# A linear-attention and feed-forward kernel: scores straddling two PSUM banks, copies of v as threads of their own, and a newly computed emission order

## The chip, the cores and the metric

The kernel runs on one core of one Trainium2 chip. The metric is the device time of one launch in microseconds (us). The times shown are of three runs of the kernel before; one more run was taken with the profiler on.

## The reference

Two layers, one behind the other. The first is a linear attention with a decaying state (4 batches, 8 heads, 768 tokens, head size 48); its output becomes a matrix of 3072 tokens by 384, and the second layer is a feed-forward block of 384 to 2048 to 384 with a gate:

```python
state = np.zeros((B, H, D, D))
for t in range(S):
    kt, vt, rt = k[:, :, t], v[:, :, t], r[:, :, t]
    cur = np.einsum('bhd,bhe->bhde', u[None] * kt, vt)
    y[:, :, t] = np.einsum('bhd,bhde->bhe', rt, state + cur)
    state = w[None, :, :, None] * state + np.einsum('bhd,bhe->bhde', kt, vt)
x = y.transpose(0, 2, 1, 3).reshape(B * S, H * D)
h = x @ w_in
sp = np.where(h > 20.0, h, np.log1p(np.exp(np.minimum(h, 20.0))))
out = (h * np.tanh(sp)) @ w_out
```

The two weight matrices are of 64-bit floats; the kernel gets them as pairs of 32-bit words.

## The kernel before, in words

**Tiling.** The tokens are worked on in 6 groups of 512 (128 tokens of each batch). A group takes 4 attention steps, one for each batch, 24 in all (s = 4 · group + batch), and then 16 hidden tiles of the feed-forward block (an "up" product of 128 hidden values by 512 tokens, a gate, a "down" product into three accumulators). In group 0 the first tiles are done in halves of 256 tokens, so that they can begin after two steps.

**One attention step** works on 128 tokens in chunks of 64. For the first steps, by name in the trace: `q` (L529, VectorE, called DVE) and the dots of r, u and k (L535, TensorE, called PE), copied out of PSUM as `sd` (L540, ScalarE, called ACT); the diagonal `P` built of `sd` (L564 on ACT in two halves of four instructions, or L566 on DVE); r and k scaled by powers of w (`scale`, L514, DVE); the scores of all pairs of tokens in a chunk (L586, PE) and a masked copy of them into `P` (L603, DVE); then `outputs`: P times v plus the carried state (`spread_y`, L636, in steps 0 to 3, `rows_y`, L661 and L673, from step 4 on), copied into x (L817, L821, L825). The keys are scaled by a table `TKn` (L578), which PE makes from a smaller one (`tkn`, L295; copied by ACT, L300). The first state of a batch is keys times v (`first_state`, L771 into `pa`, copied by L789); later steps update it (L754, L759). In steps 0 to 3 the fourth quarter of the head columns is laid out separately in a buffer `spread`, and that takes one copy of v a step (L720), which is named after the buffer that v lies in (`pre<-v`, `first<-v`, `pre<-vx`, `first<-vx`).

**The PSUM tile `pa`** has two banks of 512 columns. In both kernels it holds the scores, the sums of rows of `rows_y` (`straight`), the first states and the dots. Four PE passes of different steps thus write to the same two banks.

**The weights** arrive as 16 pieces of raw words (`wraw`), 8 of each matrix. Each piece is converted by one ACT instruction (L402) and three of DVE (L406, L408, L410), and later split into a high and a low part (L426 on ACT, L428 on DVE) for products in three passes (L892). Tiles ahead of the split use the whole value (L1014 up, L1028 down).

**What sets the order.** All engines run what the program hands them in the order in which it was emitted. A planner, the class `Flow`, computes this order when the kernel is built: each piece of work is a thread, a generator that yields names of events to wait for and costs on an engine. The planner keeps a time for each engine and takes what is ready first; among what gets ready within a margin (`PATIENCE`), a thread of a lower rank goes first if its rank is below `URGENT`. Ranks of attention steps come from `rank(s)`, those of weights from the tile that first needs them, less a lead (`L_IN`, `L_OUT`, `LAG`). `CONVERT` gives the ranks of the first conversions, `X_SPLIT` that of splitting x, `W_SHIFT` shifts the ring of weight buffers, `LO0` and `HI0` set where steps are placed among the tiles of group 0, `FETCH` the planner's price of an instruction fetch on PE. Where the planner sees PE without work, it emits filler matmuls (`keep_warm`, L310, the name `idle` in the trace), and 23 more stand at the start.

The line numbers in this section and in the prediction's quoted rows are those of the kernel before; in the kernel after, lines from 318 on stand 1 lower, those of `outputs` and what follows 7 (L586 is L587 there, L771 is L778, L1014 is L1021).

Of the kernel before, what the change touches and what calls it, by code (L numbers as in the profile page):

```python
# [21 lines left out]
B, H, S, D = 4, 8, 768, 48  # L22
NP = H // 2
C = 128
CK = C // 2
# [3 lines left out]
KT = DM // 128  # L29
# [23 lines left out]
FB = 2  # L53
COLS = FB * T
W_SLOTS = 17
W_SHIFT = 6
N_CST = CK + CK // 2


# [12 lines left out]
def split_early(w):  # L72
    return not w[0] and WG * w[1] >= FROM


def first_use(c):
    return UNITS.index((0, c) if c < AHEAD else (None, WG * c))
# [12 lines left out]
LAND0, LAND = 3.8, dict(rk=1.32, v=0.66, raw=1.96, rkn=0.5)  # L90
HT = 2 * C
FROM = 10
X_SPLIT = 0
CONVERT = (-999.5, -998.5)
LAG = 6
LO0, HI0, LO1, HI1 = 0.0, 0.85, 0.05, 0.85
LAT, LAT0 = 0.15, 0.13
WARM0, WARM_MIN, FILL = 23, 0.25, 3.25
DMA_LAT = 2.0
BLOCK0, BLOCK, FETCH, LOADING = 449, 256, 6.0, 18.0  # L100
PATIENCE = dict(dve=0.1, act=0.1, pe=0.1)
URGENT = -900
RANK = dict(token_table=-998.6, keys=-998.9, first_state=-899.5)

COST = dict(dve=1.5)
FREE = dict(pe=8.0, act=4.5, dve=2.0, pool=1.7, sp=1.0)

L_ATT, L_V, L_IN, L_OUT, L_GATE, L_EVAC, L_PUT, L_FIN = 2, -2, 7, 5, 2, 4, 9, 4


class Flow:
# [56 lines left out]
    def run(self):  # L168
        while self.live:
# [5 lines left out]
            t, th, d = min(todo[e], key=lambda t: (t[0], t[1][0]))  # L175
            soon = [o for o in todo[e] if o[0] <= t + PATIENCE.get(e, 0.0) and o[1][0] < min(th[0], URGENT)]
            if soon:
# [15 lines left out]
def act(cols):  # L193
    return {"act": 0.1 + cols / 1060}
# [6 lines left out]
def pe(us, n):  # L201
    us = Us(us)
    us.n = n
    return {"pe": us}
# [3 lines left out]
def rwkv_mish_kernel(ctx, tc, rkT, rkN, vN, wT, w_in, w_out, consts, rkF, vF, wF, uF, outT):  # L208
    nc = tc.nc
# [38 lines left out]
    loaded, marks = {}, {}  # L248
# [31 lines left out]
    spread = (pre[:, 1], pre2)  # L280
# [22 lines left out]
    flow = None  # L303

    def keep_warm(n, out=None):

        if flow:
            flow.begun += 2 * n
        for _ in range(n):
            nc.tensor.matmul(  # L310
                idle if out is None else out, lhsT=zeros.broadcast_to([128, 128]),
                rhs=zeros.broadcast_to([128, 512]), start=True, stop=True,
            )

    pa = ps.tile([128, 2, 512], F32, name="pa", tag="pa")
    for i in range(2):
        keep_warm(1, pa[:, i])
    scored = pa[:, :, : NP * CK].rearrange("j i (p t) -> j i p t", p=NP)
    straight = pa[:, :, NP * CK : (NP + 2) * CK].rearrange("m i (q t) -> m i q t", q=2)
    first_states = [pa[:, b, NP * CK : NP * (CK + D)].rearrange("d (p e) -> d p e", p=NP) for b in range(2)]  # L320
    dotted = pa[:, 0, NP * (CK + D) : NP * (CK + D) + H]
    idle = ps.tile([128, 512], F32, name="idle", tag="acc0")
    keep_warm(WARM0 - 2)

    flow = Flow(FREE, 2 * WARM0)
# [48 lines left out]

    W_ORDER = sorted(((i, f) for i in range(2) for f in range(NW)), key=lambda w: first_use(w[1]) + w[0] * W_SHIFT)
    S_ORDER = sorted(W_ORDER, key=lambda w: not split_early(w))
# [232 lines left out]
    def spread_y(s):  # L609
        rk, _, v = loaded[s][:3]  # L610
        P = Ps.pop(s)
        ys = ps.tile([128, 512], F32, name="y", tag="yt"), hp_tile("yh", f"half{s}")
        todo = [[], []]

        def add(row, j, b, k, lhsT, rhs):
            todo[row].append((j, (2 * k + b) * CK, lhsT, rhs))

        for q in range(NP) if s >= 2 else ():
            for b in range(2):
                for k in (q,) if q < KT else range(KT):  # L620
                    for j in range(2):
                        i, p = head(q, j)
                        at = 2 * (s % 2) + b
                        S = states[ROWS[i], at, p] if q < KT else spread_S[ROWS[i], at, j, k]
                        add(i, j, b, k, S, rk[ROWS[i], 0, p, HALVES[b]])
        for n in range(2 * KT):
            for j in range(2):
                for b in range(2):
                    i, p = head(min(n, KT), j)
                    lhsT = v[HALVES[b], j, n] if n < KT else spread[s % 2][HALVES[b], j, n - KT]  # L630
                    add(b, j, b, n % KT, lhsT, P[HALVES[b], 2 * p + i])
        for n in range(max(map(len, todo))):
            for row in range(2):
                if n < len(todo[row]):
                    j, at, lhsT, rhs = todo[row][n]
                    nc.tensor.matmul(  # L636
                        ys[row][HALVES[j], at : at + CK], lhsT=lhsT, rhs=rhs, start=n < 2, stop=n >= len(todo[row]) - 2
                    )
        return ys
# [55 lines left out]
    reads = [0] * NS  # L695
    stamp = const.tile([1, 1], F32, name="stamp")

    def outputs(s):
        rows, last = s >= B, s >= NS - 2
        yield f"masked{s}"  # L700
        yield f"v{s}"
        if s:
            yield f"y{s - 1}"
        if s >= 2:
            yield f"state{s - 2}"
        if rows:
            if not last:
                yield f"keys{s}"
                yield f"state{s - 1}"
            if s + 1 < NS:  # L710
                yield f"scaled{s + 1}"
            yield from hp_free()
        else:
            if s >= 2:
                yield f"out{s - 2}"
                yield f"spread{s - 2}"
            yield from hp_free()
            engine = yield {**act(96), "dve": 0.25}
            v = loaded[s][2]
            (nc.scalar.copy if engine == "act" else nc.vector.tensor_copy)(  # L720
                out=spread[s % 2][:, :, :, D:], in_=v[:, :, KT, :D].rearrange("t q (k e) -> t q k e", k=KT)
            )
        yield from paced(s, 1)
        if not rows:
            yield pe(*((0.95, 96) if s < 2 else (1.8, 192)))
            yield from hp_free(0.0)
            ys = spread_y(s)
        else:
            yield pe(2.1 - 0.4 * last, 256 - 64 * last)
            yield from hp_free(0.0)  # L730
            ys = rows_y(s, last)
        flow.set(f"out{s}")
        flow.start(finish(s, ys), rank(s) - L_FIN)
        if not rows:
            flow.start(first_state(s), s + (RANK["first_state"] if s < 2 else -899.5))
        elif not last:
            yield from update_state(s, new_states(ys))
        else:
            flow.set(f"state{s}")
# [3 lines left out]
    def new_states(ys):  # L743
        return [y[:, 2 * CK : 2 * CK + NP * D].rearrange("d (p e) -> d p e", p=NP) for y in ys[::-1]]
# [121 lines left out]
    def paced(s, piece):  # L866
        if s >= B:
            yield f"u{place(s, piece)}"

    def rank(s):  # L870
        return (place(s, 0) if s == B else place(s - 1, 1)) - L_ATT if s >= B else s - 1000
# [7 lines left out]
    def hp_free(cost=None):  # L879

        if cost is None:
            if len(hp_log) >= 2:
                yield hp_log[-2]
            return
        while len(hp_log) >= 2 and hp_log[-2] not in flow.events:
            yield hp_log[-2]
            yield pe(cost, 0)
# [299 lines left out]

    load_early()
    for s in range(NS):
        for k, thread in enumerate((load_step, load_v, scale, dots, diag, keys, attend, outputs)):  # L1190
            if thread is keys and s >= NS - 2 or s <= B and thread in (load_step, load_v):
                continue
            if thread is keys and s < B:
                flow.start(keys(s), s + (RANK["keys"] if s < 2 else -899.8), 0.0)
                continue
            flow.start(thread(s), rank(s) + k / 1000 - (L_V if s >= B and thread is load_v else 0), 0.0)
    flow.start(check_range(), 999, 0.0)
    flow.start(split_x(), X_SPLIT, 0.0)
    flow.start(load_rest(), -1200, 0.0)
    flow.start(prologue(), -1100, 0.0)  # L1200
    flow.start(token_table(), RANK["token_table"], 0.0)
    for c in range(len(W_ORDER)):
        i, f = W_ORDER[c]
        at = first_use(f) + (LAG - L_OUT if i else -L_IN) + c / 1000
        flow.start(convert(c), CONVERT[c] if c < len(CONVERT) else at, 0.0)
    for n, (i, f) in enumerate(S_ORDER):
# [12 lines left out]
    with tc.If(in_range < 128 * N_FLAGS):  # L1219
# [48 lines left out]
        with tc.tile_pool(name="any2", bufs=1) as work:  # L1268
            raw = work.tile([128, WE, 2], U32, name="raw")
            top, bottom = raw[:, :, 1], raw[:, :, 0]  # L1270
            e = work.tile([128, WE], F32, name="e")
            eu = e.bitcast(U32)
            for c, key in enumerate(W_ORDER):
# [7 lines left out]
                    out=eu, in0=top, scalar=0x80000000, in1=eu, op0=ALU.bitwise_and, op1=ALU.bitwise_xor  # L1281
# [10 lines left out]
            for b in range(B):  # L1292
                with tc.For_i(0, S, 128) as t0:
# [4 lines left out]
                    t = ps.tile([128, 512], F32, name="t", tag="yt")  # L1298
                    for k in range(KT):
                        nc.tensor.transpose(  # L1300
                            out=t[:, k * 128 : (k + 1) * 128], in_=xt[:, k].rearrange("t q e -> t (q e)"), identity=unit32
                        )
                    t = t[:, : KT * 128].rearrange("m (k t) -> m k t", k=KT)
# [81 lines left out]
```

## Time and profile before

| | us |
|---|---|
| median of 3 runs | 495.22 (495.0 to 495.71) |
| the profiled run | 494.16 |
| span in its profile, first to last instruction | 492.1 |
| PE busy | 480.5 (98% of the span) |
| ACT busy | 399.0 (81%) |
| DVE busy | 364.9 (74%) |
| first large up tile on PE starts at | 25.77 |
| first three-pass tile | 74.04 |
| first up tile of group 1 | 106.78 |

Times within a profile count from the start of the span. PE is busy nearly throughout; a lower clock of PE counts as busy too, and so does a filler matmul. "Granted clock" is the share of full speed that the chip's throttle gave PE in a stretch.

### The profile page before, as it was taken

How to read it: one execution, taken by the hardware profiler on the slowest of the kernel's cores; microseconds unless marked ns; L12 is line 12 of the kernel's file. 1: busy time of each engine (PE TensorE's matmuls, PEld its weight loads, DVE VectorE, ACT ScalarE, POOL GpSimd, SP SyncE). 2: the span in 40 equal slices, each digit the busy share in tenths (PEclk: the TensorE clock that was granted, in tenths of full speed). 3: DMA queues.
4: the chain of work that ended last, by engine and by line, in shares of the span. 5: the costliest groups of instructions: out<-in, count | busy, mean ns of one | idle time of the engine just before them, and what ended most of it. 6: DMA issues, size and time to landing. Idle time of an engine off the chain costs nothing.

```text
span 492.1 us, 11411 instructions
## 1 busy us (share of the span) xinstructions
PE 480.5 (98%) x4869; PEld 385.9 (78%) x4870; DVE 364.9 (74%) x584; ACT 399.0 (81%) x506; POOL 5.3 (1%) x28
## 2 busy tenths in 40 slices
PE   8899999999999999999999999999999999999993
PEld 4688878866678888888888888888888888888872
DVE  7899999996998665779787788875878546554531
ACT  3668999899898888886869596989787888989881
POOL 2000000000000000000000000000000000000000
PEclk9789999999999999999999999999999999999998
DMA  8792694510244030236042446142435112120002
GB/s 328 278 334 91 239 311 162 207 38 5 95 148 128 3 111 1 98 117 214 10 148 93 162 143 215 46 143 99 163 111 195 66 37 108 65 104 24 3 0 71
DMA packets 19979, 60.45 MB, mean 123 GB/s; under 512 B 3088, under 2 KB 3984, under 8 KB 19920
## 3 DMA queue, kind: packets, MB, share of 16 engines
q1 hardware_dynamic: 17184, 54.80, 32.8%
q10 hardware_dynamic: 2736, 4.84, 2.7%
q8 instruction: 40, 0.66, 0.5%
q14 instruction: 19, 0.16, 0.1%
HBM read 52.94 MB, written 4.72 MB: 117 GB/s over the span
## 4 chain that ended last, share of the span: by engine, by line
PE 93%; ACT 3%; DVE 2%; issue 1%; DMA 0%; ACTq 0%; DVEq 0%
PE hp L892 36%; PE acc L892 30%; PE acc L1028 9%; PE hp L1014 6%; PE pa L586 3%; PE yt L661 1%; PE yh L771 1%; PE pa L673 1%; PE pa L661 1%; PE pa L535 1%; PE idle L310 1%; PE yh L673 1%; PE y L636 1%; PE acc L1148 1%; ACT L919 1%
## 5 line engine op out<-in xcount | busy, mean ns | idle before, releaser
L892 PE MATMUL hp<-x,w 128*128 128x512 f32 x720 | 180.7, 395 | 0.0
L892 PEld LDWEIGHTS hp<-x,w 128*128 128x128 f32 x720 | 133.8, 188 | 30.3 <-issue 2.4
L892 PE MATMUL acc<-gh,w 128*128 128x512 f32 x468 | 156.1, 389 | 0.0
L892 PEld LDWEIGHTS acc<-gh,w 128*128 128x128 f32 x468 | 87.8, 188 | 18.3
L892 PE MATMUL acc<-gl,w 128*128 128x512 f32 x234 | 91.1, 390 | 0.0
L932 DVE TENSOR_TENSOR hb<-hb,fa 128x1024 f32<-128x1024 f32 x40 | 48.9, 1222 | 54.9 <-ACT fa L925 54.8
L919 ACT ACT_TABLE_LOAD x48 | 61.6, 1283 | 6.5 <-DVE hb L932 5.1
L925 ACT ACT_TABLE_LOAD x48 | 61.6, 1283 | 0.8
L919 ACT ACTIVATE fa<-hb,small 128x1024 f32<-128x1024 f32 x48 | 55.3, 1153 | 1.5 <-DVE hb L932 0.8
L922 ACT ACTIVATE fa<-fa 128x1024 f32<-128x1024 f32 x48 | 50.9, 1061 | 0.9
L892 PEld LDWEIGHTS acc<-gl,w 128*128 128x128 f32 x234 | 43.9, 188 | 9.5 <-DVE gl L940 0.4
L925 ACT ACTIVATE fa<-fa 128x1024 f32<-128x1024 f32 x48 | 50.9, 1060 | 0.5
L940 DVE TENSOR_TENSOR gl<-hb,gh 128x1024 fp32r<-128x1024 f32 x40 | 48.9, 1221 | 1.7 <-ACT gh L936 1.1
L1080 ACT COPY hb<-hp 128x512 f32<-128x512 f32 x55 | 32.2, 585 | 20.9 <-PE hp L892 15.2
L1080 DVE COPY hb<-hp 128x512 f32<-128x512 f32 x41 | 28.3, 690 | 25.2 <-PE hp L892 23.7
L1028 PE MATMUL acc<-gf,wraw 128*128 128x256 f32 (+1 forms) x144 | 44.4, 453 | 0.0
L1028 PEld LDWEIGHTS acc<-gf,wraw 128*128 128x128 f32 x144 | 27.9, 196 | 10.5 <-issue 7.7
L936 ACT CAST gh<-hb 128x1024 fp32r<-128x1024 f32 x14 | 14.7, 1053 | 20.0 <-DVE hb L932 19.9
L1014 PE MATMUL hp<-x,wraw 128*128 128x256 f32 (+1 forms) x108 | 28.9, 420 | 0.0
L514 DVE TENSOR_TENSOR rk<-rk,TRK 112x1024 f32<-112x1024 f32 x22 | 26.8, 1220 | 0.6 <-DMA rk<-in_rkT_dram 0.6
L1014 PEld LDWEIGHTS hp<-x,wraw 128*128 128x128 f32 x108 | 21.5, 204 | 4.3 <-issue 1.9
L936 DVE CAST gh<-hb 128x1024 fp32r<-128x1024 f32 x26 | 18.0, 694 | 2.3 <-PE acc L892 0.2
(140 smaller groups left out, 569.5 us busy)
## 6 DMA issues: line engine op xcount, KB each, us to landing
wraw<-in_w_in_dram SPq DMA_DIRECT2D x16, 768.0 KB, 4.5
wraw<-in_w_out_dram SPq DMA_DIRECT2D x16, 768.0 KB, 4.7
rk<-in_rkT_dram SPq DMA_DIRECT2D x22, 512.0 KB, 4.5
rkn<-in_rkN_dram SPq DMA_DIRECT2D x20, 384.0 KB, 4.8
v<-in_vN_dram SPq DMA_DIRECT2D x22, 256.0 KB, 4.9
out_dram<-ob ACTq DMA_DIRECT2D x12, 256.0 KB, 2.2
x<-x SPq DMA_DIRECT2D x60, 32.0 KB, 1.9
out_dram<-we ACTq DMA_DIRECT2D x5, 256.0 KB, 4.8
```

The costliest lines, as they stand in the source:

```text
L514: marks[f"scaled{s}"] = nc.vector.tensor_tensor(out=rk[:112].rearrange("d a p (b t) -> d (a p) b t", b=2), in0=rk[:112].rearrange("d a p ( ...
L586: nc.tensor.matmul(scored[h, i, p], lhsT=rk[ROWS[i], 1, p, h], rhs=rk[ROWS[i], 0, p, h], start=True, stop=True)
L892: nc.tensor.matmul(out, lhsT=a, rhs=m, start=first and n == 0, stop=last and n == 2)
L919: nc.scalar.activation(o.g, o.hb, AF.Sigmoid, bias=bias_ln2, scale=1.0)
L922: nc.scalar.activation(o.g, o.g, AF.Arctan)
L925: nc.scalar.activation(o.g, o.g, AF.Sin, scale=2.0)
L932: nc.vector.tensor_tensor(out=o.hb, in0=o.hb, in1=o.g, op=ALU.mult)
L936: (nc.scalar.copy if engine == "act" else nc.vector.tensor_copy)(out=o.gh, in_=o.hb)
L940: nc.vector.tensor_tensor(out=o.gl, in0=o.hb, in1=o.gh.bitcast(F32), op=ALU.subtract)
L1014: nc.tensor.matmul(hp[:, at], lhsT=whole[0, f // WG][:, fs], rhs=xs[0][:, k, steps, 0], start=k == 0, stop=k == KT - 1)
L1028: nc.tensor.matmul(accs[mt][:, at], lhsT=whole[1, f // WG][:, ws], rhs=g[:, of], start=not n and not i, stop=n == NF - 1, skip_group_check ...
L1080: (nc.scalar.copy if engine == "act" else nc.vector.tensor_copy)(out=o.hb[:, j], in_=h)
```

## The change

Four edits. First, the columns of `pa`: each bank is seen as two quarters of 256 columns. The scores go to the second quarter of bank 0 and the first of bank 1, which lie next to each other, 512 columns in one piece; row sums and first states go to the outer quarters, the dots from bank 0 to the end of bank 1. Second, the copy of v into `spread` in steps 0 to 3 is taken out of `outputs` and made a thread, which can go as soon as v is there and the buffer is free. Third, constants of the planner. Fourth, with these the order of emission comes out anew.

```diff
-W_SHIFT = 6
+W_SHIFT = 4
...
-X_SPLIT = 0
-CONVERT = (-999.5, -998.5)
+X_SPLIT = 4
+CONVERT = (-998.4, -997.4, -996.4, -995.4)
...
-LO0, HI0, LO1, HI1 = 0.0, 0.85, 0.05, 0.85
+LO0, HI0, LO1, HI1 = 0.05, 0.80, 0.05, 0.85
...
-BLOCK0, BLOCK, FETCH, LOADING = 449, 256, 6.0, 18.0
+BLOCK0, BLOCK, FETCH, LOADING = 449, 256, 4.5, 18.0
...
-URGENT = -900
+URGENT = 1000
...
-L_ATT, L_V, L_IN, L_OUT, L_GATE, L_EVAC, L_PUT, L_FIN = 2, -2, 7, 5, 2, 4, 9, 4
+L_ATT, L_V, L_IN, L_OUT, L_GATE, L_EVAC, L_PUT, L_FIN = 3, -2, 8, 6, 2, 4, 9, 4
...
-    scored = pa[:, :, : NP * CK].rearrange("j i (p t) -> j i p t", p=NP)
-    straight = pa[:, :, NP * CK : (NP + 2) * CK].rearrange("m i (q t) -> m i q t", q=2)
-    first_states = [pa[:, b, NP * CK : NP * (CK + D)].rearrange("d (p e) -> d p e", p=NP) for b in range(2)]
-    dotted = pa[:, 0, NP * (CK + D) : NP * (CK + D) + H]
+    quarters = pa.rearrange("j i (h c) -> j (i h) c", h=2)
+    scored = quarters[:, 1:3].rearrange("j i (p t) -> j i p t", p=NP)
+    straight = quarters[:, ::3, : 2 * CK].rearrange("m i (q t) -> m i q t", q=2)
+    first_states = [quarters[:, 3 * b, : NP * D].rearrange("d (p e) -> d p e", p=NP) for b in range(2)]
+    dotted = quarters[:, 3, NP * D : NP * D + H]
...
+    def spread_v(s):
+        if s >= 2:
+            yield f"out{s - 2}"
+        yield f"v{s}"
+        engine = yield {**act(96), "dve": 0.25}
+        v = loaded[s][2]
+        (nc.scalar.copy if engine == "act" else nc.vector.tensor_copy)(
+            out=spread[s % 2][:, :, :, D:], in_=v[:, :, KT, :D].rearrange("t q (k e) -> t q k e", k=KT)
+        )
+        flow.set(f"spread_v{s}")
+
     def outputs(s):
...
+            yield f"spread_v{s}"
             if s >= 2:
-                yield f"out{s - 2}"
                 yield f"spread{s - 2}"
             yield from hp_free()
-            engine = yield {**act(96), "dve": 0.25}
-            v = loaded[s][2]
-            (nc.scalar.copy if engine == "act" else nc.vector.tensor_copy)(
-                out=spread[s % 2][:, :, :, D:], in_=v[:, :, KT, :D].rearrange("t q (k e) -> t q k e", k=KT)
-            )
...
     for s in range(NS):
+        if s < B:
+            flow.start(spread_v(s), rank(s) + 0.0045, 0.0)
```

Where the order changes, three places count. The first is PE just behind the outputs of step 0, before (the last matmul of those outputs, `P` times `pre`; the table `tkn`; dots and scores of step 2; the outputs of step 1):

```order
L636 MATMUL yh<-P,pre 64x64
L295 MATMUL tkn<-pre,TRK 64x96 x8
L535 MATMUL pa<-cst,q 128x2 x4
L586 MATMUL pa<-first 64x64 x16
L636 MATMUL y<-P,v 64x64
L636 MATMUL yh<-P,v 64x64
```

In the new order the table stands ahead of step 0's outputs, and behind them come scores 1, dots 2 and the first state of step 0 (`pa<-v,kn`), then fillers:

```order
L637 MATMUL yh<-P,pre 64x64
L587 MATMUL pa<-rk 64x64 x16
L536 MATMUL pa<-cst,q 128x2 x4
L778 MATMUL pa<-v,kn 48x48 x16
L310 LDWEIGHTS zeros
L310 MATMUL idle<-zeros 128x512
```

First state 0 has moved from behind the dots of step 3 to here, and the scores of step 2 have gone from here to behind step 1's outputs. The number of fillers between step 0's scores and the first up tile falls from 11 to 7.

The second place is PE around the first up tile (`hp<-x,wraw`), before. Here stand the dots of step 3, first state 0 and the scores of step 3, and the tile behind them:

```order
L636 MATMUL yh<-P,first 64x64
L535 MATMUL pa<-cst,q 128x2 x4
L771 MATMUL pa<-v,kn 48x48 x16
L586 MATMUL pa<-first 64x64 x16
L1014 MATMUL hp<-x_285,wraw 128x256 x6
L636 MATMUL y<-first,S 64x64
```

In the new order scores 2 and dots 3 come first, and the scores of step 3 stand behind the tile:

```order
L637 MATMUL yh<-P,first 64x64
L587 MATMUL pa<-first 64x64 x16
L536 MATMUL pa<-cst,q 128x2 x4
L1021 MATMUL hp<-x_267,wraw 128x256 x6
L587 MATMUL pa<-first 64x64 x16
L637 MATMUL y<-first,S 64x64
```

So the tile no longer stands behind the scores of step 3, nor directly behind the first state.

The third place is ACT from the copy of the table `TKn` on, before (dots copy `sd` and diagonal `P` of step 2, a weight conversion, the outputs of step 1 into x, the dots copy of step 3, the first state):

```order
L300 COPY TKn<-tkn 128x384
L720 COPY first<-v 128x6x16
L540 COPY sd<-pa 128x8
L564 ACTIVATE P<-cst,sd 128x64 x8
L402 ACTIVATE wraw<-wraw 128x768
L817 COPY x_285<-y 128x3x64
L817 COPY x_285<-yh 128x3x64
L540 COPY sd<-pa 128x8
L789 COPY S<-pa 112x4x48
L402 ACTIVATE wraw<-wraw 128x768
```

In the new order the table's copy stands between the halves of step 1's diagonal, and the conversion and the state copy between the halves of step 2's:

```order
L565 ACTIVATE P<-cst,sd 128x64 x4
L300 COPY TKn<-tkn 128x384
L565 ACTIVATE P<-cst,sd 128x64 x4
L824 COPY x_267<-y 128x3x64
L705 COPY pre<-vx 128x6x16
L824 COPY x_267<-yh 128x3x64
L541 COPY sd<-pa 128x8
L403 ACTIVATE wraw<-wraw 128x768
L565 ACTIVATE P<-cst,sd 128x64 x4
L796 COPY S<-pa 112x4x48
L565 ACTIVATE P<-cst,sd 128x64 x4
```

The copies of v that stood behind the table's copy have moved ahead; the state copy `S<-pa` now stands ahead of step 1's copies into x, in the middle of step 2's diagonal.

The first group's later part has two more moves on PE: hidden tile 8 and one set of down products stand ahead of step 4 instead of behind it, and the first tile in three passes (`hp<-xp,w`) ahead of step 5 instead of behind it. On DVE the split of that tile's weights (L428) stands directly behind step 4's state update. From the second group on PE's order is the same, but for a small matmul of the check on the weights' range, which moves by one tile; the last part of the order is the same on PE, ACT and DVE.

## The prediction

> **What bounds the kernel now.** I read the page first, then the busy time in stretches, then the rows of the first 40 us engine by engine. The page of the kernel before gives the span, the share of TensorE (PE), its slices, the granted clock, and the chain that ended last:
>
> ```profile
> span 492.1 us, 11411 instructions
> PE 480.5 (98%) x4869; PEld 385.9 (78%) x4870; DVE 364.9 (74%) x584; ACT 399.0 (81%) x506; POOL 5.3 (1%) x28
> ...
> PE   8899999999999999999999999999999999999993
> ...
> PEclk9789999999999999999999999999999999999998
> ...
> PE 93%; ACT 3%; DVE 2%; issue 1%; DMA 0%; ACTq 0%; DVEq 0%
> ```
>
> PE is busy for 480.5 of 492.1 us, and the chain is PE for 93%. So time can only be won where PE stands idle, does filler work, or runs at a lower clock. The first three slices and the last show all of that there is. The order of the tail is unchanged by the edit, so the start decides. In stretches of 3.4 us the start reads as follows (columns: stretch and its length, then busy time and count of PE, weight loads, DVE, ACT, POOL, then the granted clock, DMA share, GB/s); the last row is the rest of the first token group:
>
> ```profile
> core 0: us, PE busy (x) PEld busy (x) DVE busy (x) ACT busy (x) POOL busy (x), PEclk, DMA share, GB/s
> 0.70:4.10 3.40, 3.15 (x8) 1.19 (x9) 0.93 (x4) 1.49 (x2) 3.27 (x3) 1.00 0.61 198
> ...
> 7.50:10.90 3.40, 2.83 (x49) 2.35 (x49) 3.37 (x7) 1.27 (x6) 0.00 (x0) 1.00 1.05 402
> 10.90:14.30 3.40, 3.40 (x12) 1.47 (x12) 3.40 (x6) 3.37 (x15) 0.00 (x0) 0.50 1.02 408
> 14.30:17.70 3.40, 3.40 (x106) 2.78 (x104) 3.34 (x7) 2.11 (x6) 0.00 (x0) 0.99 0.74 274
> 17.70:21.15 3.45, 1.94 (x83) 1.64 (x82) 2.94 (x6) 2.44 (x11) 0.00 (x0) 1.00 0.66 233
> 21.15:24.55 3.40, 2.69 (x40) 2.52 (x40) 2.09 (x3) 1.01 (x4) 0.00 (x0) 0.50 0.85 257
> 24.55:27.95 3.40, 3.24 (x37) 2.77 (x38) 2.38 (x5) 1.94 (x6) 0.00 (x0) 0.50 0.94 374
> ...
> 26.00:123.00 97.00, 97.00 (x1276) 76.24 (x1277) 90.62 (x148) 85.68 (x120) 0.44 (x5) 0.99 0.49 171
> ```
>
> Two things stand here. First, from 26 us on PE is never idle (97.00 of 97.00). Second, the clock is whole or half in steps of 3.4 us, and it follows the busy share of the stretch before: after 3.15 and 3.40 busy it is whole; after 2.83, 1.94 and 2.69 it is half; after 3.24 it is whole from 27.95 on. I use that as this trace's rule: over about 3.1 of 3.4 us busy, the next stretch is whole.
>
> The PE rows between step 1 and the first big tiles (start, length, then the instructions, then idle time ahead of them and its cause):
>
> ```profile
> 10.22 1.20 PE L535 MATMUL pa<-cst,q 112*128 112x2 f32 x8
> 11.28 3.60 PE L310 MATMUL idle<-zeros 128*128 128x512 bf16 x9
> 14.81 0.69 PE L586 MATMUL pa<-rk 48*64 48x64 f32 x32
> 15.32 0.22 PE L636 MATMUL y<-P,v 64*64 64x64 f32 x1
> ...
> 16.13 0.88 PE L295 MATMUL tkn<-pre,TRK 112*64 112x96 f32 x16
> 16.94 1.05 PE L535 MATMUL pa<-cst,q 112*128 112x2 f32 x8
> 17.93 0.69 PE L586 MATMUL pa<-first 48*64 48x64 f32 x32
> ...
> 19.20 0.27 PE L636 MATMUL yh<-P,v 64*64 64x64 f32 x1 [0.49 <-issue]
> ...
> 21.73 1.87 PE L535 MATMUL pa<-cst,q 112*128 112x2 f32 x8 [1.61 <-DVE P L603]
> 23.53 0.90 PE L771 MATMUL pa<-v,kn 64*48 64x48 f32 x32
> 24.71 1.14 PE L586 MATMUL pa<-first 48*64 48x64 f32 x32 [0.28 <-ACT sd L540]
> 25.77 3.93 PE L1014 MATMUL hp<-x,wraw 128*128 128x256 f32 x12
> ...
> 31.79 5.46 PE L1014 MATMUL hp<-x,wraw 128*128 128x256 f32 x24
> ...
> 38.96 2.87 PE L1014 MATMUL hp<-x,wraw 128*128 128x256 f32 x12
> ```
>
> From 11.28 to 14.81 PE does nine filler matmuls, .39 us each at half clock. At 21.73 the dots of step 3 have waited 1.61 us for step 2's masked copy. Dots, first state, scores and part of the first up tile then run at half clock (dots 1.87 against 1.05 at 16.94; the tile 3.93 against 2.87). Tiles 1 and 2 start at 31.79; from there PE runs through in both kernels, so I measure the change at that point.
>
> ACT and DVE around it:
>
> ```profile
> 13.24 1.06 ACT L564 ACTIVATE P<-cst,sd 128x64 f32<-128x64 bf16 x4
> ...
> 17.06 0.48 ACT L300 COPY TKn<-tkn 128x384 f32<-128x384 f32 x1 [0.27 <-PE tkn L295]
> ...
> 18.69 0.17 ACT L540 COPY sd<-pa 128x8 f32<-128x8 f32 x1 [0.98 <-PE pa L586]
> ...
> 20.81 0.89 ACT L402 ACTIVATE wraw<-wraw 128x768 f32<-128x768 uint32 x1
> ```
>
> ```profile
> 17.07 0.68 DVE L529 TENSOR_TENSOR q<-first 112x512 f32<-112x512 f32 x1
> 17.67 0.55 DVE L578 TENSOR_TENSOR kn<-kn,TKn 128x384 f32<-128x384 f32 x1
> 18.14 0.95 DVE L408 SCALAR_TENSOR_TENSOR we<-wraw,we 128x768 uint32<-128x768 uint32 x1
> ...
> 20.94 0.73 DVE L603 COPY_PREDICATED P<-cst,pa 128x512 f32<-128x512 uint32 x1 [0.51 <-ACT P L564]
> 21.57 1.21 DVE L514 TENSOR_TENSOR first<-first,TRK 112x1024 f32<-112x1024 f32 x1
> ```
>
> **The change part by part.** *New columns.* The scores, the state products and the dots still lie in the two banks of one tile, and they stay ordered by bank: after the change the copy of the dots still waits for the scores, as at 18.69 (0.98, released by the scores, which write other columns than it reads). Worth 0; at most the 0.28 of 24.71, at least 0, since no pass is added.
>
> *Copies of v as threads.* Four copies of 96 columns either way; three on ACT and one on DVE before and after. They come earlier, where ACT waits for its first dots. Worth 0.
>
> *Constants.* They matter through the order. From the second group on PE's order is the same but for the one small matmul of the range check. In the first group tile 8 and the first three-pass tile come earlier against steps 4 and 5; PE is busy there throughout and its matmuls are the same, so 0, while ACT and DVE keep up (the rival below prices it).
>
> *The start.* Four fillers fewer (11 become 7 after step 0's scores), the token table ahead of step 0's outputs, first state 0 and the dots of step 3 earlier, scores 3 behind the first up tile. I walk the new order with the rows above, start to start:
> - PE: dots 1 as before to 11.3; 3 fillers at half clock 1.2 (12.5); table, half clock, some 1.3 (13.8); 2 fillers .6 (14.4); outputs 0 .81 (15.2); scores 1 .51 (15.7); dots 2 .99 (16.7); first state 0, .6 (17.3), since 0.90 was at half clock. Its keys need the table's copy, 13.8 + .48, then .47 on DVE: 14.8, in time.
> - DVE's masked copy 1 now waits for that first state: 17.35 + .63 = 18.0. ACT: dots copy 18.2, weight conversion .83 (19.05), half of the diagonal .96 (20.0), state copy .3 (20.3). PE's scores 2 wait for that state copy, in the same banks: 20.35 to 20.9. Queued on DVE behind the masked copy: scale 2 1.15, keys .47, a shift .46, q 3 .60, to 20.7. Dots 3 start at 20.9; from 21.15 at half clock, since the stretch 17.70 to 21.15 holds about 1.9 us of PE work (outputs 1, with its .49 stall, then a gap of 1 us): 1.75, to 22.65.
> - Up tile 0 starts at 22.65 against 25.77. The stretch 21.15 to 24.55 is now full of PE work (dots 3, then the tile), 3.3 to 3.4 us instead of 2.69, so by the rule the clock is whole from 24.55, not 27.95. The tile is 2.84 us of whole-clock work (2.18 us at half clock and 1.75 whole before): 1.90 us at half speed do .95, the other 1.89 end at 26.45.
> - Scores 3 .5 (26.95); their scaled keys are due at 22.7 + .63 + .95 + 1.15 = 25.4, in time. Outputs 2 and first state 1 took 31.79 − 29.70 = 2.09: tiles 1 and 2 start at 29.05.
>
> The gain is 31.79 − 29.05 = 2.7 us. It splits into 1.9 from an earlier first tile with scores 3 behind it, and .85 from the earlier whole clock. Before's profiled run took 494.16 us (2.06 around its span), 1.06 under the median of the three runs shown. The sum, 494.16 − 2.7 = 491.4 against that run, is 492.5 against the median 495.22.
>
> **A rule of the skill against the trace.** Half clock here follows stretches with gaps of at most 1.61 us. The Trainium skill, "TensorE: Matmul & The Clock Gate", section "Why this matters for your kernels", says that drops are avoided when no idle gap of PE exceeds about 3 us; by it the new start would never fall to half clock. The same page of the Trainium skill, Part 1, tells of a free-running window of about 3.4 us, and with that the trace agrees (steps of 3.4 us); on the gap it doesn't, since 2.83 busy of 3.40, with no gap over half a microsecond, was already followed by half clock.
>
> **The rivals.**
> 1. *The clock stays whole throughout.* Speaks for it: the fillers and the earlier work could lift the stretch before 21.15 over the mark. Against: my walk has 1.9 us busy there. Then dots 3 end at 21.9, the tile at 24.8, and masked copy 3 on DVE (27.05) holds first state 1: tiles 1 and 2 at 27.7, gain 4.1, time 491.1. By the Trainium skill's gap rule just named this would be the case.
> 2. *Half clock until 27.95 as before*, because eight dots of two columns don't count as busy, or the steps lie elsewhere against the program. For: 2.69 busy, mostly dots and first state, was not enough. Against: 3.24 was, and the new stretch has more. Then the tile ends at 28.15, tiles 1 and 2 start at 30.75: gain 1.0, time 494.2.
> 3. *Half clock in 14.30 to 17.70 too*, since five fillers and the table replace nine fillers. PE's 3.1 us of work from 14.3 then end 1.7 later, at 19.0, and all behind it shifts: dots 3 end near 24.8, the tile at 29.3, tiles 1 and 2 at 31.8: gain 0, time 495.2. Against: 10.90 to 14.30 has no gap in my walk.
> 4. *It doesn't do what it says.* The columns free no wait (as at 18.69), and the reordered waits on the banks (masked copy 1 for first state 0, scores 2 for the state copy) cost what they save: 495.2.
> 5. *Slower: the first three-pass tile waits.* It now stands ahead of step 5 on PE, about 2.0 us of PE work earlier, besides the 2.7. These rows show its weights made on DVE and its use:
>
> ```profile
> 69.65 0.95 DVE L428 TENSOR_TENSOR w<-wraw,w 128x768 fp32r<-128x768 f32 x1
> ...
> 74.04 2.20 PE L892 MATMUL hp<-xp,w 128*128 128x512 f32 x8
> ```
>
> The tile would be due at 74.04 − 4.7 = 69.3. Were the weights made as late as now (70.6), PE would wait 1.3 of the 2.7 gained. It decides from weights at 72.0; at 73.0 the kernel is .2% slower, 496.2. For it: DVE idles only 6.4 of 97 us, and must also do more of the conversions. Against: DVE's new order puts that split right behind step 4's state update, near 66.
>
> **How the numbers follow.** A change of .2%, 1.0 us, is about what can be told from none. Chances: forecast .50 (492.5), rival 1 .07 (491.1), rival 2 .15 (494.2, on the line between faster and same), rival 3 .11, rival 4 .08 (both 495.2), rival 5 .09 (496.2 or more). Faster: .50 + .07 + half of .15 = .65. Same: the other half + .11 + .08 = .26. Slower: .09. The range leaves out rival 5 and half of rivals 3 and 4 above (.19) and little below: 491.1 to 495.2. The forecast's own range is 491.9 to 493.2 (.6 either way for the handoffs that I read at under .1 us each).
>
> **What would show it.** Right: the first up tile starts near 22.7 and tiles 1 and 2 near 29; the clock is half only in 10.9 to 14.3 and 21.2 to 24.6; 7 fillers after step 0's scores; no wait of PE before the dots of step 3 on a masked copy, but one of about 1 us before scores 2, released by ACT's state copy; PE without idle time in the rest of the first group; same tail. Wrong: half clock at 25 to 28 (rival 2) or 15 to 17 (rival 3), PE waits before the first three-pass tile (rival 5), or a start as late as before.

## The result, and the profile after

The change made the kernel slower: 499.66 us (median of 20 runs, 494.2 to 501.88) against 496.05 us before (20 runs, 494.38 to 497.52), a ratio of 1.0061 with a 95% interval of 1.0043 to 1.008. I had forecast 492.5 us, faster. The profiled run of the changed kernel took 495.84 us, one of its quicker ones, so its trace holds the causes but less than their usual cost. Ratios and their intervals, here and below, are as recorded and not the quotients of the medians; they leave out slow runs, those over 1.5% above the fastest of their kernel (501.88 here, 544.76 us with 40 instructions more, 806.15 us with one load earlier).

The waits of PE in the changed kernel (what waited and for what: us in total, times, longest):

```profile
PE hp L1021 <- issue: 3.3, 1, 3.3
PE pa L310 <- DVE small L233: 0.9, 1, 0.9
PE pa L536 <- DVE q L530: 0.7, 1, 0.7
PE yh L637 <- issue: 0.6, 1, 0.6
...
PE pa L587 <- ACT S L796: 0.2, 1, 0.2
```

The wait for step 2's masked copy (1.61 us before) is gone, and one of 3.3 us has taken its place, ahead of an up tile, released by nothing that the trace shows ("issue"). The PE rows of the start show where it lies:

```profile
14.50 0.65 PE L587 MATMUL pa<-rk 48*64 48x64 f32 x32
15.08 1.05 PE L536 MATMUL pa<-cst,q 112*128 112x2 f32 x8
16.06 0.58 PE L778 MATMUL pa<-v,kn 64*48 64x48 f32 x32
...
20.33 1.05 PE L536 MATMUL pa<-cst,q 112*128 112x2 f32 x8
21.26 2.87 PE L1021 MATMUL hp<-x,wraw 128*128 128x256 f32 x12
24.29 0.70 PE L587 MATMUL pa<-first 48*64 48x64 f32 x32 [0.17 <-issue]
27.04 0.58 PE L778 MATMUL pa<-v,kn 64*48 64x48 f32 x32 [0.42 <-DVE P L604]
30.90 8.34 PE L1021 MATMUL hp<-x,wraw 128*128 128x256 f32 x24 [3.29 <-issue]
40.97 2.87 PE L1021 MATMUL hp<-x,wraw 128*128 128x256 f32 x12
```

The new start is fast: the first up tile begins at 21.26 (25.77 before), first state 1 ends at 27.6. Tiles 1 and 2 could follow 4 us earlier than before's 31.79. PE stands until 30.90 instead, and then the two tiles take 8.34 us (5.46 before). The stretches of this run, cut where its clock steps, show why (columns as before):

```profile
9.49:12.90 3.41, 2.67 (x54) 2.06 (x55) 2.99 (x6) 2.72 (x12) 0.00 (x0) 1.00 1.06 417
12.90:16.32 3.42, 3.42 (x120) 2.79 (x119) 3.37 (x5) 2.54 (x11) 0.00 (x0) 1.00 1.03 404
16.32:19.73 3.41, 1.97 (x82) 1.33 (x72) 2.96 (x5) 2.20 (x8) 0.00 (x0) 1.00 0.54 149
19.73:23.14 3.41, 3.41 (x49) 3.19 (x50) 2.93 (x5) 2.36 (x10) 0.00 (x0) 1.00 0.40 164
...
26.56:29.97 3.41, 0.64 (x35) 0.45 (x32) 3.38 (x7) 1.91 (x5) 0.00 (x0) 1.00 0.88 300
29.97:33.38 3.41, 2.48 (x6) 2.03 (x7) 3.10 (x5) 1.38 (x3) 0.00 (x0) 0.50 1.00 416
33.38:36.80 3.42, 3.42 (x10) 2.71 (x9) 1.38 (x2) 0.37 (x1) 0.00 (x0) 0.50 1.02 416
```

After the stretch with .64 us of PE work the clock is half for two stretches. A gap of 3.3 us and some 3 us of slower tiles outweigh the 4 us won.

All runs list their span and mean granted clock, and that separates the two causes. Span times clock is the span as if the half-clock time had run at full speed; it varies little, while the rest of the spread is half-clock time, 2 · (1 − clock) · span. The split is rough, since a clock that is half while PE stands counts too:

| kernel | span x clock, mean us | time at half clock, median us |
|---|---|---|
| before (runs beside the experiments) | 486.5 to 486.9 | about 14 |
| changed (20 runs; 12 more) | 488.6; 488.9 | 17.9; 16.9 |

So about 2 us of the loss (1.7 to 2.4) are idle time or work, and about 2 us (half of some 4 us) are clock. For example a run of 494.2 us had a clock of .991 (8.9 us at half), one of 501.55 us one of .979 (21 us).

### The profile page after: what moved, and what is told of

Its sections match the earlier page's. It is cut to its first block, busy times and chain, and to the rows that moved or that the text cites. A ratio compares the mean times of both kernels' runs of the same rounds, so it can differ in the third digit from the quotient of the medians.

```text
span 493.9 us, 11405 instructions
## 1 busy us (share of the span) xinstructions
PE 479.3 (97%) x4864; PEld 385.3 (78%) x4866; DVE 363.7 (74%) x580; ACT 399.3 (81%) x510; POOL 5.3 (1%) x28
## 4 chain that ended last, share of the span: by engine, by line
PE 90%; ACT 3%; DMA 2%; DVE 1%; issue 1%; SPq 0%; ACTq 0%; DVEq 0%
PE hp L899 36%; PE acc L899 30%; PE acc L1035 8%; PE hp L1021 6%; PE pa L587 2%; DMA rk<-in_rkT_dram 1%; PE yt L662 1%; PE yh L778 1%; PE pa L674 1%; PE pa L662 1%; DMA wraw<-in_w_in_dram 1%; PE yh L674 1%; PE pa L536 1%; PE acc L1155 1%; ACT L926 1%
## 5 line engine op out<-in xcount | busy, mean ns | idle before, releaser
L899 PE MATMUL hp<-x,w 128*128 128x512 f32 x720 | 180.8, 396 | 0.0
L899 PEld LDWEIGHTS hp<-x,w 128*128 128x128 f32 x720 | 133.9, 188 | 30.2 <-issue 2.1
L899 PE MATMUL acc<-gh,w 128*128 128x512 f32 x468 | 156.2, 389 | 0.0
L899 PEld LDWEIGHTS acc<-gh,w 128*128 128x128 f32 x468 | 87.9, 188 | 18.2
L899 PE MATMUL acc<-gl,w 128*128 128x512 f32 x234 | 91.2, 390 | 0.0
L899 PEld LDWEIGHTS acc<-gl,w 128*128 128x128 f32 x234 | 43.9, 188 | 9.5 <-DVE gl L947 0.4
L1087 DVE COPY hb<-hp 128x512 f32<-128x512 f32 x40 | 27.6, 690 | 23.0 <-PE hp L899 21.4
L1021 PE MATMUL hp<-x,wraw 128*128 128x256 f32 (+1 forms) x108 | 30.9, 442 | 3.3 <-issue 3.3
L1021 PEld LDWEIGHTS hp<-x,wraw 128*128 128x128 f32 x108 | 22.6, 215 | 8.1 <-issue 5.3
L352 DVE TENSOR_REDUCE small<-we 128x1 f32<-128x768 f32 x16 | 15.2, 949 | 10.9 <-ACT we L350 10.9
```

The source lines that it names most:

```text
L352: v.tensor_reduce(out=to[:, 0:1], in_=e, axis=AX.X, op=ALU.min)
L899: nc.tensor.matmul(out, lhsT=a, rhs=m, start=first and n == 0, stop=last and n == 2)
L1021: nc.tensor.matmul(hp[:, at], lhsT=whole[0, f // WG][:, fs], rhs=xs[0][:, k, steps, 0], start=k == 0, stop=k == KT - 1)
```

## The experiments

Three explanations stood against each other: F, the gap is the fetch of PE's instructions; W, it is a wait of the program that the profile misnames; B, the new columns cost time in every step. For F speaks a row of the DMA records: in a window of 1.1 us in the gap there is one packet of 16 KB on the instruction queue, and none in the 6 us ahead of it (queue and kind: packets, MB, share):

```profile
q8 instruction: 1, 0.02, 5.6%
```

If an instruction takes 64 bytes, 16 KB are 256 of them, the planner's own `BLOCK`; the runs below test that. The 40 packets of this queue in the whole run would make 10240 instructions, about as many as the profile counts of PE (9730).

**The changed kernel once more.**

> The changed kernel once more, for a second profile. Theory F (instruction fetch): the start of the new order is as fast as walked, but PE then stands for 2 to 5 us ahead of up tiles 1 and 2 with no releaser in the trace, until a 16 KB packet of the instruction queue has landed about 1.3 us before; the gap lets the clock fall, and the spread of the runs is time at half clock (about 10 us of it in a run of 496, about 18 to 21 us in a run of 499 to 501). Rival W: the gap is a wait of the program that the profile fails to name (a weight's conversion, a copy into x). Rival B: the two-bank columns cost time in every step.

Measured: 499.06 us (12 runs), ratio 1.0062 (1.0034 to 1.0089). In its profile the gap is there, 2.32 us, after a start that was 1.7 us later. As F has it.

**The columns alone.** The diff of the columns, as shown, on the kernel before.

> The kernel before with the new columns of the PSUM tile alone; its order of emission is the same, instruction for instruction. Theory F: no difference, ratio 1.000 within 0.002. Rival B: slower by the 3.6 us that the whole change lost, or a good part of them.

Measured: 496.38 against 495.83, ratio 1.0016 (1.0005 to 1.0027). Not the 3.6 us that were lost, so B falls as the main cause; but not quite nothing either.

**84 more instructions ahead of everything.**

```diff
-    keep_warm(WARM0 - 2)
+    keep_warm(WARM0 - 8)
+    for _ in range(48):
+        nc.tensor.matmul(idle[:, :32], lhsT=zeros.broadcast_to([128, 128]),
+                         rhs=zeros.broadcast_to([128, 32]), start=True, stop=True)
```

> The changed kernel, with 6 of the 21 wide filler matmuls at the very start replaced by 48 narrow ones (32 columns) of about the same time together: 42 matmuls and their weight loads, 84 PE instructions, more ahead of everything, and nothing else moved. Theory F: the borders of the instruction blocks (256 instructions of 64 bytes) come 84 instructions earlier in the program, the block with up tile 1 is asked for 2 to 3 us earlier (during the first up tile instead of behind it), and the gap ahead of tiles 1 and 2 shrinks from 3.3 to under 1.5 us or vanishes; time 3 to 6 us less than the changed kernel's 499.7. Rival W: the gap stays at 3 us where it is, time 499 to 500.

Measured: 494.02 us, ratio .9958 (.9941 to .9975): 5 us less than the changed kernel, with more filler instructions in about the same time. Span times clock falls from 488.9 to 485.4. Its PE rows show no gap ahead of the tiles:

```profile
32.72 0.56 PE L782 MATMUL pa<-v,kn 64*48 64x48 f32 x28
33.20 5.46 PE L1025 MATMUL hp<-x,wraw 128*128 128x256 f32 x24
```

**A whole block more.** The same with 15 wide fillers out and 143 narrow ones in, 256 instructions.

> The changed kernel with 15 of the wide fillers at the very start replaced by 143 narrow ones (32 columns): 128 matmuls with their weight loads, 256 PE instructions, more, one whole block of instructions, so that the borders of the blocks stand where they stand without any shift. Theory F (borders of blocks of 256): the gap ahead of tiles 1 and 2 is back, 2 to 3.5 us; span times clock back at 488 to 489; time 497 to 501. Rival N (not the borders but something else about the narrow fillers, such as an earlier first matmul or a warmer clock, made shift84 5 us faster): no gap, 493 to 495.

Measured: 500.33 us, ratio 1.0068 (1.0038 to 1.0098). The gap is back in its place, and with it span times clock (488.4):

```profile
32.52 0.56 PE L782 MATMUL pa<-v,kn 64*48 64x48 f32 x28
36.81 7.14 PE L1025 MATMUL hp<-x,wraw 128*128 128x256 f32 x24 [3.73 <-issue]
```

That the effect has a period of 256 instructions, and that the narrow fillers by themselves help nothing, is the clearest evidence for F. A count of PE's instructions in the traces (matmuls, weight loads and those of its sequencer, in order of their start) says the same. Each gap that F claims, in this run and the others, stands ahead of an instruction within two of the 449th or the 961st, which are two blocks apart. At the 449th are .49 us in the kernel before, .62 in the changed one and .66 with 40 more; at the 961st 3.29 in the changed one, 2.32 in its second profile and 1.71 with 40 more. With 256 more the latter gap stands at the 1219th, a block further on. The planner's constants `BLOCK0, BLOCK = 449, 256` put the borders there too.

**Forty instructions more** (3 wide out, 23 narrow in), to see whether the gap moves with the border.

> The changed kernel with 3 wide fillers replaced by 23 narrow ones: 20 matmuls with their weight loads, 40 PE instructions, more. Theory F: the border that lay right ahead of tiles 1 and 2 now lies 40 instructions earlier, which is inside first state 1 (64 instructions, which end there): the gap starts after about 12 of its 32 matmuls and no longer behind them; it is asked for at nearly the same time (scores 3 lie there, dense), so its length stays 2 to 3.5 us, time 497 to 501. Rival W (a wait of tiles 1 and 2): the gap stays directly ahead of the tiles.

Measured: the gap is inside first state 1, after 4 + 8 = 12 of its 32 matmuls, as forecast:

```profile
32.55 0.24 PE L782 MATMUL pa<-v,kn 64*48 64x48 f32 x1
...
32.73 0.37 PE L782 MATMUL pa<-v,kn 64*48 64x48 f32 x8
34.81 0.47 PE L782 MATMUL pa<-v,kn 64*48 64x48 f32 x20 [1.71 <-issue]
35.21 5.46 PE L1025 MATMUL hp<-x,wraw 128*128 128x256 f32 x24
```

Nothing in the profile ties the thirteenth of these matmuls to anything, so W falls. Its length, 1.71, is under the 2 to 3.5 that I gave, and so is the time, 496.63 us, ratio 1.0004 (.9985 to 1.0022).

**The shift on the kernel before.**

> The kernel before with the 84 additional PE instructions of shift84. Theory F: there the block came just in time (its packet had landed at 30.1, tiles 1 and 2 began at 31.8), and PE was held by other waits, so that little is to be won: 495 to 496, ratio 0.998 to 1.001. Rival N: the shift alone gives what shift84 gained over the kernel before, 493.5 to 494.3. Possible loss under F: a border falls in another dense stretch, up to 3 us.

Measured: 496.57 against 496.1, ratio .9998 (.9982 to 1.0014). The shift is worth nothing there; what it frees in the changed kernel is the changed order's own gain.

**The shift with old columns,** and **128 instructions with old columns** (8 wide out, 72 narrow in), and **the changed kernel with old columns.**

> shift84 with the old columns of the two-bank tile; the order of emission is the same. Where the columns do nothing: 494.0, the same as shift84. Where they cost what the comparison with the columns alone suggests (ratio 1.0016): 493.2.

> The changed kernel with old columns and 128 more PE instructions (8 wide fillers become 72 narrow). Theory F: the border lies inside the outputs of step 2, asked for before the first up tile; the gap is under 1 us, and time is 492 to 494, as with 84. If the earlier border now meets another dense stretch: a gap of 1 to 2 us there, 494 to 496.

> The changed kernel with the old columns; order of emission the same. Columns inert: 499.5 +- 0.7. Columns costing 0.8 us as between shift84 and its twin: 498.5. The gap ahead of tiles 1 and 2 stays.

Measured: 493.02 us, ratio .9937 (.9914 to .996), the best of all; 494.05, ratio .9959 (.9944 to .9974), no gap, the time just above the 492 to 494 given; 498.73, ratio 1.004 (1.0009 to 1.0071), gap 4.19 us. In the last one the profile names a releaser for the gap:

```profile
PE hp L1020 <- ACT first L801: 4.2, 1, 4.2
```

The tile doesn't read what that copy writes, and in the changed kernel the same copy ran at 31.79, after the tile had begun: a coincidence of time. The gap stands ahead of the 961st instruction here too.

**The planner's price of a fetch.** `FETCH` back from 4.5 to 6.0 in the changed kernel.

> The changed kernel with one constant undone: the planner's price of an instruction fetch back at 6.0 from 4.5; the order is computed anew, and in it the first up tile stands behind the outputs of step 2 instead of ahead of them. Theory F: the planner then counts with the gap that the trace shows (fetch to resumption some 5 to 6 us) and puts other work in it; PE's gap is smaller, 494 to 497, faster than the changed kernel. Rival: the gap stays ahead of the next tiles and costs the same, 499 to 500.

Measured: 497.96 us, ratio 1.0035 (1.0017 to 1.0054), just outside the range given, and 1.7 us under the changed kernel. The fetch gap is gone, but PE waits in other places:

```profile
PE hp L1021 <- ACT hb L1087: 2.4, 1, 2.4
PE pa L587 <- ACT S L796: 2.1, 1, 2.1
```

**The copies of v alone.** `spread_v` and its start, as in the diff, on the kernel before.

> The kernel before with the copies of v as threads and nothing else; the order is computed anew, and in it scores 3 stand behind the first up tile, as in the whole change, while the table, the fillers and first state 0 stay where they were. Theory F: the start is won only in part, the block is asked for later than in the whole change relative to PE's need, gap 0 to 2 us, time 494.5 to 497.5. Should the copies alone carry the loss of the whole change: 499 to 500.

Measured: 498.91 us, ratio 1.0077 (1.0049 to 1.0104). I had given 494.5 to 497.5; this part alone loses as much as the whole change. The gap is there, after 29 of first state 1's 32 matmuls, and PE waits for x in a later tile:

```profile
PE pa L777 <- issue: 1.7, 1, 1.7
PE hp L898 <- DMA x<-x: 1.6, 2, 1.4
```

**Why the block is late.** One load released earlier:

```diff
-    marks[after].ins.name
+    marks["scaled2" if s == 3 else after].ins.name
```

> The changed kernel with one load of raw weights (768 KB, the fourth piece) released by scale 2 instead of by the second piece's conversion, some 4.5 us earlier, when the DMA engines stand idle; the order of all engines is the same. Theory F: 1.9 us of transfers less stand in the DMA queues when the block is asked for, and the gap shrinks by 1 to 2 us; time 1 to 5 us less than the changed kernel. Rival W with a weight as the cause: the gap shrinks too, if the awaited weight is this one; otherwise no change. Rival B: no change.

Measured: 498.06 us, ratio 1.0052 (1.0031 to 1.0074), span times clock 488.0 against 488.9; gap 2.51. By the time alone this is inconclusive. Three loads moved:

```diff
-    ("raw", 3, "whole1"), ("raw", 4, "scaled3"), ("raw", 5, "masked2"),
+    ("raw", 3, "scaled2"), ("raw", 4, "masked3"), ("raw", 5, "masked3"),
```

> The changed kernel with three loads of raw weights (768 KB each) released elsewhere: the fourth piece by scale 2 instead of the second piece's conversion (some 5 us earlier), the fifth and sixth by masked copy 3 instead of scale 3 and masked copy 2 (2 to 4 us later). The order is computed anew; up to and with up tile 1 it is the same on PE, behind it some tiles change places. So the block ahead of tile 1 is asked for when little stands in the DMA queues. Theory F1 (the block is late because it queues behind the weight loads): its packet starts 2 to 3 us earlier against PE's scores 3, the gap ahead of tile 1 falls under 1 us; time up to 5 us less than the changed kernel. F2 (a fetch takes this long whatever the queues hold): the gap stays at 2 to 4 us; time 498 to 501, apart from what the moved tiles do.

> The same three loads moved in the kernel with 84 more PE instructions and old columns (493.0 without). Under F1 and F2 alike the gap is gone there already: 492 to 494; slower if the later loads hold up the conversions.

Measured: 503.43 us, ratio 1.0142 (1.0112 to 1.0172), and 503.93, ratio 1.0151 (1.0126 to 1.0176). As times both forecasts failed: the weights now come too late (PE waits for their split, `hp L899 <- ACT w L427`, 1.1 us, and more; a wait of 2.79 us ahead of an up tile at 67.75 is named "issue" as well, yet stands at no border, so the name alone doesn't make a fetch). But the gap ahead of tile 1 did what F1 says in the first of the two:

```profile
32.52 2.87 PE L1021 MATMUL hp<-x,wraw 128*128 128x256 f32 x12 [0.63 <-ACT x L828]
```

In the second, with 84 more, no gap stands there, but one of 1.37 us ("issue") stands among the dots of step 2, at the 449th instruction and 1.50 us after a packet had landed (17.86). Without the moved loads that packet started at 13.14, here at 16.77. Why it came late here isn't known.

The packet's times in the DMA records, beside the start of scores 3 (the last tile of work ahead of the dense run of small matmuls in which the next block is asked for; that moment itself is not in the trace), with the DMA share of the 16 engines in between:

| kernel | scores 3 start | packet starts, lands | after scores 3 | DMA share | PE goes on | gap |
|---|---|---|---|---|---|---|
| before | 24.71 | 29.11, 30.07 | 4.40 | .91 | 31.79 | none |
| changed | 24.29 | 28.47, 29.45 | 4.18 | .81 | 30.90 | 3.29 |
| changed, again | 26.02 | 29.93, 30.93 | 3.91 | .73 | 32.26 | 2.32 |
| 256 more | 30.34 | 34.30, 35.21 | 3.96 | .88 | 36.81 | 3.73 |
| changed, old columns | 28.91 | 33.42, 34.39 | 4.51 | .82 | 35.78 | 4.19 |
| one load earlier | 28.91 | 32.05, 33.01 | 3.14 | .96 | 34.25 | 2.51 |
| copies of v alone | 29.55 | 31.27, 32.69 | 1.72 | .34 | 33.93 | 1.70 |
| three loads moved | 29.12 | 30.18, 31.14 | 1.06 | .00 | 32.52 | .63 |

With scores 3 behind the first up tile, as in all rows but the first, the packet starts 1.06 us behind that mark with idle DMA engines, 1.72 with a third of them busy, and 3.1 to 4.5 with loads under way. Where PE has stood, it goes on 1.2 to 1.6 us after the packet has landed. The first row can't be compared by this mark, since the first up tile (3.93 us) stands between scores 3 and the dense run there. Counted in instructions, the border ahead of the one in question is the 705th. The kernel before reaches it at 28.90, within that tile, and the packet starts .2 us later; the changed kernel reaches it at 24.77, within scores 3, and the packet starts 3.7 us later; with three loads moved, at 29.68 and .5 us later. So the loads make the delay, as the changed kernel against the one with three loads moved shows, in one profile each; how the queues share the engines isn't shown.

## Why the prediction was wrong, point by point

**The step that failed** is the one that closed the account at 31.79: "from there PE runs through in both kernels, so I measure the change at that point". What PE is handed was taken as unlimited. Scores 3, the outputs of step 2 and first state 1 are 64 + 192 + 64 instructions and take some 3.3 us on PE (24.29 to 27.62): more than a block of 256, in less time than the next needs to come. In the kernel before, the block had landed at 30.07 and PE went over the border at 31.59, 1.52 us later, which is no more than PE takes after a landing where it has stood: the fetch was a hidden second bound with next to nothing in hand. The changed kernel reached the border ahead of it 4.1 us earlier, but with the loads in the DMA queues the packet started only .6 us earlier (28.47 against 29.11). What the order had won ended there, in a gap of 3.29 us (4.19 with old columns, in a run of 498.87 us). The trace of before showed the sign, which I quoted and passed over: `[0.49 <-issue]` at 19.20, two blocks earlier in the program and 1.3 us after a packet of that queue had landed (17.89); and the diff changed a constant that prices this very fetch.

**The start.** In the two profiles of the changed kernel the walk held: 22.65 for the first up tile against 21.26 and 22.98, copy of the table between the halves of the diagonal, wait of PE for ACT's state copy ahead of scores 2 (.24 and 1.09 us, I had about 1). Without the gap, tiles 1 and 2 would have begun at 27.6 and 29.9, around the 29.05 forecast. But both were quick runs (495.84 and 495.9 us), so the agreement is in part luck: in the other profiles with the same order of PE up to there, the first up tile starts at 23.5 to 26.4, and the clock is half for 3.4 us or more between 20 and 31, as rival 2 had it in kind. With the border moved, the order's gain shows: shift84 is 1.8 us faster than before, its twin with old columns 3.1; I had 2.7.

**The clock.** The rule that I drew from the trace of before, that over 3.1 of 3.4 us busy decide, failed in the first profile: 2.67 and 1.97 busy were followed by whole clock. There rival 1 was right, and so was the rule of the Trainium skill, "TensorE: Matmul & The Clock Gate", "Why this matters for your kernels": no drop without a gap near 3 us, and a drop during one (half from 29.97 on, 2.4 us into the gap of 3.29, with .64 busy in the stretch before). But in the trace of before, and in that of shift84 with old columns (a clock of .88 over the first 26 us with gaps of at most 1.3 us), the clock fell without such a gap. In the changed kernel's second profile 1.92 us busy in 8.19 to 11.61 were followed by half clock and 1.84 in 18.43 to 21.85 by whole. What decides in between stays open. The drop at the gap was a cost that no term of mine held. The median run's longer time at half clock is worth about 2 us; how much of it lies behind the gap isn't known.

**New columns, worth 0:** they may cost a little. In three pairs with the same order, new against old, the medians are 496.38 and 495.83, 494.02 and 493.02, 499.06 and 498.73. Only the first pair was run side by side (.05 to .27%); the ratios of the others to the kernel before have overlapping intervals, and by span times clock they don't differ that way (485.4 and 485.9, 488.9 and 488.8). A cause isn't known; I had allowed no cost.

**Copies of v as threads, worth 0:** wrong by name. A thread more makes another order, and this one alone loses 3.2 us; its profile has 1.7 us of the same gap and 1.6 us of waits for x. The remainder wasn't taken apart, nor what the copies themselves cost.

**Rivals.** Rival 1's start came true in one profile, without its gain. Rival 5 had the sign, but its place shows no wait: none stands for the first three-pass tile in the changed kernel. Rivals 2 and 3 describe the clock of single runs (half from 22.46 to 29.29 with one load earlier, from 11.51 to 18.33 with old columns). The loss came by a mechanism that was not on the list.

## What to carry to other kernels

Where PE runs hundreds of small matmuls in a few microseconds, count instructions as well as time: the supply of blocks of 256 can be the bound that a faster order runs into, and a wait named "issue" at one border says that the next may be as near. Before a reordering is costed, look how long ago the next block had landed; a few fillers more or fewer far ahead can then be worth more than the order (5 us here). A stall can be a clock event too: behind the gaps of 2.32, 3.29, 3.73 and 4.19 us the next tiles ran at half clock for a stretch or two, behind those of 1.71 and 2.51 us they didn't.

## What the runs showed of the hardware

- PE's instructions come in packets of 16 KB, each about 1 us long. Where PE has stood for one, it goes on 1.2 to 1.6 us after it has landed.
- A gap's place moved by exactly the number of instructions added ahead (40), the gap went with 84 and 128, and it came back with 256.
- The packets wait behind data loads: behind the start of scores 3 one starts after 1.06 us with idle DMA engines and after 3.1 to 4.5 us with loads under way.
- The spread of this kernel's runs (494.2 to 501.9 us, a standard deviation of 2.2) is for the most part time at half clock, between 8.9 and 21 us a run; span times clock has a standard deviation of .4 to .8 us.
